# Attention times values for 448 queries in tiles of 128: the last 64 queries of two heads in one stationary operand

## Chip, cores, metric

The kernel runs on one core of a Trainium2 chip. The metric is the device time of a whole execution in microseconds. The kernel before took 406.42 us (median of 4 runs, 406.06 to 406.82). PE is TensorE, PEld its weight loads, DVE VectorE, ACT ScalarE, POOL GpSimd. The kernel places the tiles named `ps_...` and `sc`, which take PE's results here, in PSUM and all other tiles in SBUF.

## The reference

```python
def _attn_ref(q, k, v, tau):                      # 8 x 12 heads, 448 queries, 64 wide
    q_n = q / (norm(q, axis=-1) + 1e-06)
    k_n = k / (norm(k, axis=-1) + 1e-06)
    attn = softmax(q_n @ k_n.T / tau)             # its sum gets + 1e-9
    return attn @ v
# then, on x = (3584 tokens, 768):
    a = x @ w1;  b = x @ w2
    out = ((a * b) @ w3) @ w_out                  # 768 -> 1024 -> 1024 -> 768
```

## The kernel before

Heads are taken in pairs, 48 in all. POOL squares and scales q and k (`sq`, `nrm`), PE transposes them and makes the scores, ACT takes the exponentials, PE multiplies them with the values ("AV"), DVE divides by the row sums, PE transposes back, and the feed-forward part (groups `a`, `b`, `o`) fills PE in between. A planner in the kernel puts all steps in a fixed order per engine, from estimated durations.

AV has the exponentials as the stationary operand, 128 queries at a time, and the values of one head with a column of ones (65 columns) as the moving one. 448 is three and a half times 128, so the fourth tile starts at 320 and computes 64 queries a second time.

```python
QT = (0, 128, 256, S - 128)                       # S = 448, P = 112, NJ = 4, D = 64
...
def scores(pp, half):
    if half == 0:
        exps[pp] = exp_pool.tile([P, NJ, 2, S], BF16, tag="exp", name="expT")
    ...
def exp(pp, c):
    nc.scalar.activation(exps[pp][:, c], scs.pop((pp, c))[:P, :, :S], ACT.Exp,
                         scale=1.0 / float(tau))

def av(pp, hh):
    ...
    ps = psA.tile([128, NJ, D + 1], FP32, tag="av", name="ps_av")
    for m, q0 in enumerate(QT):
        for c in range(NJ):
            nc.tensor.matmul(ps[:, m, :], exps[pp][:, c, hh, q0:q0 + 128],
                             vt[:, 2 * i + hh, c, :], start=(c == 0), stop=(c == NJ - 1))
    ...
def av_norm(pp, hh):
    ps = pav.pop((pp, hh))
    rs = st_pool.tile([128, NJ, 1], FP32, tag="rs", name="rs")
    nc.vector.reciprocal(rs[:, :, 0], ps[:, :, D])
    nc.vector.tensor_mul(osds[pp][:, :, hh, :], ps[:, :, :D],
                         rs.to_broadcast([128, NJ, D]))

def trback(pp):                                   # four transposes into ps_tb
    ...
def tb_copy(pp):
    nc.vector.tensor_copy(xts[b][:, blk, :], pst.pop(("b", pp))[:, 0, :S])
```

Of the kernel before, what the change touches and what calls it, by code (L numbers as in the profile page):

```python
# [8 lines left out]
FP32 = mybir.dt.float32  # L9
BF16 = mybir.dt.bfloat16  # L10
AX = mybir.AxisListType
ALU = mybir.AluOpType
ACT = mybir.ActivationFunctionType
# [6 lines left out]
class Plan:  # L20
# [22 lines left out]
    def add(self, name, on, rank, emit, after=(), takes=(), holds=(), kb=0, later=None,  # L43
            until=None, slack=0.0, port=False):
        self.steps[name] = dict(on=on, rank=rank, emit=emit, after=list(after), later=later,
                                takes=list(takes), kb=kb, until=until, slack=slack, port=port)
        for key in holds:
            self.holders.setdefault(key, []).append(name)
# [79 lines left out]
def kernel(  # L128
# [12 lines left out]
    nc = tc.nc  # L141

    B, H, S, D = q.shape
# [3 lines left out]
    P = 112  # L147
    NJ = S // P
# [5 lines left out]
    KO2 = DF // 128  # L154
    NH = DM // 2
    NP = B * NPAIR
    QT = (0, 128, 256, S - 128)

    ctx.enter_context(tc.manual_schedule())

    const = ctx.enter_context(tc.tile_pool(name="const", bufs=1))
    wpool = ctx.enter_context(tc.tile_pool(name="wpool", bufs=1))
    raw_pool = ctx.enter_context(tc.tile_pool(name="raw", bufs=3))
    sq_pool = ctx.enter_context(tc.tile_pool(name="sq", bufs=3))
    st_pool = ctx.enter_context(tc.tile_pool(name="st", bufs=3))
    nrm_pool = ctx.enter_context(tc.tile_pool(name="nrm", bufs=3))
    head_pool = ctx.enter_context(tc.tile_pool(name="head", bufs=2))
    exp_pool = ctx.enter_context(tc.tile_pool(name="exp", bufs=3))
# [5 lines left out]
    psA = ctx.enter_context(tc.tile_pool(name="psA", bufs=1, space=PSUM))  # L174
# [85 lines left out]
    qks, exps, osds, xts, pst, scs, pav = {}, {}, {}, {}, {}, {}, {}  # L260

    def tr(pp):
        g, i = divmod(pp, GP)
        n = nrms[g]
        ps = psT.tile([128, 2, 512], BF16, tag="tr", name="ps_tr")
        for t in range(2):
            for j in range(NJ):
                nc.tensor.transpose(  # L268
                    ps[:, t, j * P:(j + 1) * P],
                    n[:, i, t, j].rearrange("p h d -> p (h d)"),  # L270
                    ident[:P, :P])
        qks[pp] = head_pool.tile([128, 2, S], BF16, tag="qkT", name="qkT")
        pst[pp] = ps

    def tr_copy(pp):
        nc.vector.tensor_copy(qks[pp], pst.pop(pp)[:, :, :S])  # L276

    def scores(pp, half):
        if half == 0:
            exps[pp] = exp_pool.tile([P, NJ, 2, S], BF16, tag="exp", name="expT")  # L280
        for c in (2 * half, 2 * half + 1):
            sc = psS.tile([128, 2, 512], FP32, tag="sc", name="sc")
            for hh in range(2):
                nc.tensor.matmul(  # L284
                    sc[:P, hh, :S],
                    qks[pp][64 * hh:64 * hh + 64, 1, c * P:(c + 1) * P],
                    qks[pp][64 * hh:64 * hh + 64, 0, :],
                    start=True, stop=True)
            scs[pp, c] = sc

    def exp(pp, c):
        nc.scalar.activation(exps[pp][:, c], scs.pop((pp, c))[:P, :, :S], ACT.Exp,  # L292
                             scale=1.0 / float(tau))

    def av(pp, hh):
        g, i = divmod(pp, GP)
        vt = v_tiles[g % NV]
        ps = psA.tile([128, NJ, D + 1], FP32, tag="av", name="ps_av")
        for m, q0 in enumerate(QT):
            for c in range(NJ):  # L300
                nc.tensor.matmul(  # L301
                    ps[:, m, :],
                    exps[pp][:, c, hh, q0:q0 + 128],
                    vt[:, 2 * i + hh, c, :],
                    start=(c == 0), stop=(c == NJ - 1))
        if hh == 0:
            osds[pp] = head_pool.tile([128, NJ, 2, D], BF16, tag="osd", name="osd")
        pav[pp, hh] = ps

    def av_norm(pp, hh):  # L310
        ps = pav.pop((pp, hh))
        rs = st_pool.tile([128, NJ, 1], FP32, tag="rs", name="rs")
        nc.vector.reciprocal(rs[:, :, 0], ps[:, :, D])  # L313
        nc.vector.tensor_mul(osds[pp][:, :, hh, :], ps[:, :, :D],  # L314
                             rs.to_broadcast([128, NJ, D]))

    def trback(pp):
        b, blk = divmod(pp, NPAIR)
        if blk == 0:
            xts[b] = xpool.tile([128, NPAIR, S], BF16, tag="xT", name="xT")  # L320
        ps = psT.tile([128, 2, 512], BF16, tag="tr", name="ps_tb")
        for m, q0 in enumerate(QT):
            nc.tensor.transpose(  # L323
                ps[:, 0, q0:q0 + 128],
                osds[pp][:, m].rearrange("p h d -> p (h d)"), ident)
        pst["b", pp] = ps

    def tb_copy(pp):
        b, blk = divmod(pp, NPAIR)
        nc.vector.tensor_copy(xts[b][:, blk, :], pst.pop(("b", pp))[:, 0, :S])  # L330

    abts = {}

# [88 lines left out]
    warm_sb = const.tile([128, 512], BF16, name="warm_sb")  # L422
    nc.vector.memset(warm_sb, 0.0)
    ident = const.tile([128, 128], BF16)

    def warm():
        ps = psM.tile([128, 512], FP32, tag="pm", name="ps_warm")
        for _ in range(2):
            nc.tensor.matmul(ps[:, :S], warm_sb[:, :128], warm_sb[:, :S], start=True, stop=True)

    def ones():
        for t in v_tiles:
            nc.gpsimd.memset(t[:, :, :, D:D + 1], 1.0)
# [4 lines left out]
                   exp=3, xT=2, a_sb=KO2, big=1, out_sb=3),  # L438
        begin=dict(PE=1.0, ACT=3.0, DVE=1.2, POOL=1.3))
    add = plan.add  # L440

    add("ident", [("POOL", 0.6)], -90, lambda e: make_identity(nc, ident), later="wo0")
    add("ones", [("POOL", 0.45)], -70, lambda e: ones())
    every = slice(None)
    w3_part = [slice(k, k + 2) for k in range(0, KO2, 2)]
# [10 lines left out]
    for name in loads:  # L456
# [5 lines left out]
        else:  # L462
# [5 lines left out]
            else:  # L468
                i, h0 = "qk".index(what), 2 if g == 0 else 0
# [11 lines left out]
    def chain(what, p, t):  # L481
        return f"{what}{p}.0" if t else f"{what}{p - 1}.1" if p else None
# [8 lines left out]
    for g in range(NG):  # L491
        for i in range(GP):
            p = g * GP + i
            for t in range(2):
# [4 lines left out]
                else:  # L499
# [8 lines left out]
                    holds=[("sq", p, t)], later=chain("sum", p, t),  # L508
# [7 lines left out]
        for i0, i1 in parts:  # L516
            ps = range(g * GP + i0, g * GP + i1)
# [11 lines left out]
    for p in range(NP):  # L529
        g, i = divmod(p, GP)  # L530
        b, blk = divmod(p, NPAIR)
        last = p > 0
        add(f"tr{p}", [("PE", 0.42)], p - 1.2, lambda e, p=p: tr(p),
            [f"scale{p}.0", f"scale{p}.1", "ident"] + ([f"tr{p - 1}"] if last else []),
            [("tr", ("tr", p)), ("qkT", ("qkT", p))], [("nrm", g)],
            slack=0.3 if g > 2 else 0.0)
        add(f"ev{p}", [("DVE", 0.54)], p - 1.1, lambda e, p=p: tr_copy(p), [f"tr{p}"],
            holds=[("tr", p)])
        for h in range(2):
            add(f"sc{p}.{h}", [("PE", 0.6)], p + 0.5 * h - 1, lambda e, p=p, h=h: scores(p, h),  # L540
                [f"ev{p}"] + ([f"sc{p}.0"] if h else [f"sc{p - 1}.1"] if last else []),
                [("sc", ("sc", p, 2 * h)), ("sc", ("sc", p, 2 * h + 1))]
                + ([] if h else [("exp", ("exp", p))]), [("qkT", p)])
            for c in (2 * h, 2 * h + 1):
                add(f"exp{p}.{c}", [("ACT", 0.82)], p + 0.25 * c - 1,
                    lambda e, p=p, c=c: exp(p, c),
                    [f"sc{p}.{h}"] + ([f"exp{p}.{c - 1}"] if c else []), holds=[("sc", p, c)])
        for h in range(2):
            add(f"av{p}.{h}", [("PE", 0.53)], p + 0.5 * h, lambda e, p=p, h=h: av(p, h),
                [f"exp{p}.{c}" for c in range(NJ)] + [f"spread{g}"]  # L550
                + ([f"av{p}.0"] if h else [f"av{p - 1}.1"] if last else []),
                [("av", ("av", p, h))] + ([] if h else [("osd", ("osd", p))]),
                [("exp", p), ("vt", g)])
            add(f"an{p}.{h}", [("DVE", 0.62)], p + 0.5 * h - 0.5,
                lambda e, p=p, h=h: av_norm(p, h), [f"av{p}.{h}"], holds=[("av", p, h)])
        add(f"tb{p}", [("PE", 0.24)], p + 1, lambda e, p=p: trback(p),
            [f"an{p}.0", f"an{p}.1"] + ([f"tb{p - 1}"] if last else []),
            [("tr", ("tb", p))] + ([] if blk else [("xT", ("xT", b))]), [("osd", p)])
        add(f"xt{p}", [("DVE", 0.31)], p - 0.2, lambda e, p=p: tb_copy(p), [f"tb{p}"],
            holds=[("tb", p)])  # L560

    line = []
# [52 lines left out]
    for n in range(60):  # L615
        add(f"warm{n}", [("PE", 0.4)], 10000 + n, lambda e: warm(),
            takes=[("pm", ("warm", n))], later=f"warm{n - 1}" if n else None, until=11.0)
# [39 lines left out]
```

## Time and profile before

| kernel before | |
|---|---|
| time | 406.42 us |
| profiled span, mean granted PE clock | 404.3 us, 0.994 |
| busy PE / DVE / ACT / POOL | 395 / 216 / 248 / 246 us |
| AV matmuls per pair, start to start | 32, 32.5 ns each |
| one exponential (112 x 896) | 916 ns |
| visible PE holes after the first 12 us | 3.4 us in all |

The lines are in the prediction below. How to read them: a group row has the source line, engine, operation, output and inputs, sizes and count, then busy time and the mean of one, then the idle time in front of the group and what ended it. The matmuls of a group overlap in the records (the 16 AV matmuls that start at 209.27 us have a record of 0.68 us, and the next group starts after 0.52), so the cost of a group on PE is the distance from its start to the next start in the timeline. The granted clock is a reading of the profile, as a share of PE's full speed. PE is the bound here (395 of 404.3 us busy), so busy time of another engine matters only where PE waits for it.

### The profile page before, as it was taken

The numbers are of one execution on the slowest core, as the hardware profiler recorded it, in microseconds if no ns is written. First come the engines' busy times: TensorE is split into PE (matmuls) and PEld (weight loads), VectorE is DVE, ScalarE is ACT, GpSimd is POOL, SyncE is SP. The second block draws the span as 40 slices with busy tenths as digits, with TensorE's granted clock in tenths as the row PEclk, the third lists the DMA queues.
The fourth block names the chain that finished last, engine by engine and source line by source line (L and its number), as shares of the span: only waits on it lengthen the run. The fifth ranks groups of instructions, "written<-read, shape, count | busy, mean of one in ns | idle before, by whom it ended". The sixth has DMA issues, their size and how long they took to land.

```text
span 404.3 us, 9387 instructions
## 1 busy us (share of the span) xinstructions
PE 395.0 (98%) x3944; PEld 234.9 (58%) x3944; DVE 216.3 (53%) x484; ACT 247.9 (61%) x399; POOL 245.9 (61%) x258
## 2 busy tenths in 40 slices
PE   8799999999999999999999999999999999999995
PEld 3466665556555666555655566556655566555553
DVE  2785647587576755766655766444344443420310
ACT  3687777766676676757776757566656676323222
POOL 7479899999999999999999999315100000000000
PEclk9899999999999999999999999999999999999999
DMA  8999999256585285753745365000210013103005
GB/s 144 201 206 207 210 199 153 36 70 104 119 102 71 36 153 113 101 68 36 141 82 70 38 106 123 30 2 2 79 39 2 2 41 84 36 0 105 14 5 153
DMA packets 42474, 35.18 MB, mean 87 GB/s; under 512 B 1856, under 2 KB 36416, under 8 KB 42432
## 3 DMA queue, kind: packets, MB, share of 16 engines
q0 software_dynamic: 37312, 23.11, 41.0%
q1 hardware_dynamic: 4752, 11.07, 9.4%
q8 instruction: 31, 0.51, 0.5%
q10 hardware_dynamic: 368, 0.40, 0.3%
q14 instruction: 11, 0.09, 0.1%
HBM read 46.66 MB, written 11.01 MB: 143 GB/s over the span
## 4 chain that ended last, share of the span: by engine, by line
PE 73%; POOL 19%; DMA 3%; issue 2%; DVE 1%; ACT 0%; POOLq 0%; DVEq 0%
PE ps_b L336 15%; PE ps_a L336 14%; PE ps_o L336 14%; PE ps_av L301 10%; PE sc L284 9%; POOL sq L229 8%; POOL nrm L255 7%; PE ps_w L336 5%; PE ps_tr L268 4%; DMA wo_sb<-in_moe_w_out_dram 3%; PE ps_tb L323 2%; POOL raw L198 2%; POOL v_sb L214 2%; PE ps_w L349 1%; POOL w_sb L217 0%
## 5 line engine op out<-in xcount | busy, mean ns | idle before, releaser
L292 ACT ACTIVATE expT<-sc 112x896 bf16<-112x896 f32 x192 | 166.0, 916 | 43.2 <-PE sc L284 42.9
L336 PEld LDWEIGHTS <-w_sb 128*128 128x128 bf16 x768 | 69.6, 98 | 57.2 <-issue 4.1
L255 POOL TENSOR_TENSOR nrm<-raw,rn 112x512 bf16<-112x512 bf16 x90 | 90.8, 1036 | 2.2 <-PE ps_tr L268 2.1
L229 POOL TENSOR_TENSOR sq<-raw 112x512 bf16<-112x512 bf16 x87 | 87.8, 1037 | 0.2
L336 PE MATMUL ps_b<-xT,w_sb 128*128 128x448 bf16 x384 | 83.2, 353 | 0.0
L336 PE MATMUL ps_a<-xT,w_sb 128*128 128x448 bf16 x384 | 83.0, 352 | 0.0
L336 PE MATMUL ps_o<-w_sb,abT 128*128 128x384 bf16 x448 | 80.1, 326 | 0.0
L235 DVE TENSOR_REDUCE ss<-sq 112x8 f32<-112x512 bf16 x96 | 64.0, 679 | 15.2 <-POOL sq L229 14.9
L382 DVE TENSOR_TENSOR abT<-a_sb,ps_b 128x448 bf16<-128x448 bf16 x64 | 39.6, 619 | 57.7 <-PE ps_b L336 54.8
L301 PEld LDWEIGHTS <-expT 112*128 112x128 bf16 x1536 | 59.2, 98 | 19.4 <-issue 8.8
L371 ACT CAST a_sb<-ps_a 128x448 bf16<-128x448 f32 x64 | 34.0, 532 | 52.4 <-PE ps_a L336 51.5
L301 PE MATMUL ps_av<-v_sb,expT 112*128 112x65 bf16 x1536 | 65.2, 194 | 0.0
L284 PE MATMUL sc<-qkT 64*112 64x448 bf16 x384 | 56.9, 374 | 1.4 <-DVE qkT L276 1.3
L336 PEld LDWEIGHTS <-abT 128*128 128x128 bf16 x448 | 41.3, 98 | 26.5 <-issue 2.7
L342 ACT COPY out_sb<-ps_o 128x384 f32<-128x384 f32 x43 | 20.6, 478 | 38.0 <-PE ps_o L336 36.5
L314 DVE TENSOR_TENSOR osd<-ps_av,rs 128x256 bf16<-128x256 f32 x96 | 40.7, 424 | 3.3
L313 DVE RECIPROCAL rs<-ps_av 128x4 f32<-128x4 f32 x96 | 17.1, 178 | 46.2 <-PE ps_av L301 45.9
L214 POOL COPY v_sb<-vraw 112x1536 bf16<-112x1536 bf16 x16 | 23.4, 1460 | 24.4 <-PE ps_av L301 24.0
L276 DVE COPY qkT<-ps_tr 128x896 bf16<-128x896 bf16 x48 | 29.7, 619 | 12.1 <-PE ps_tr L268 12.1
L330 DVE COPY xT<-ps_tb 128x448 bf16<-128x448 bf16 x48 | 18.6, 387 | 20.5 <-PE ps_tb L323 20.2
L284 PEld LDWEIGHTS <-qkT 64*112 64x112 bf16 x384 | 17.3, 125 | 20.7 <-issue 16.4
L268 PEld LDWEIGHTS <-nrm 112*128 112x128 bf16 x384 | 21.9, 99 | 12.1 <-issue 6.6
(37 smaller groups left out, 220.3 us busy)
## 6 DMA issues: line engine op xcount, KB each, us to landing
vraw<-in_v_dram POOLq DMA_DIRECT2D x16, 336.0 KB, 4.8
raw<-in_q_dram POOLq DMA_DIRECT2D x15, 336.0 KB, 5.6
raw<-in_k_dram POOLq DMA_DIRECT2D x15, 336.0 KB, 7.6
w_sb<-in_moe_w_dram POOLq DMA_DIRECT2D x2, 1536.0 KB, 25.4
out_dram<-out_sb SPq DMA_DIRECT2D x7, 336.0 KB, 2.8
out_dram<-out_sb SPq DMA_DIRECT2D x8, 288.0 KB, 3.0
w_sb<-in_moe_w_dram POOLq DMA_DIRECT2D x4, 512.0 KB, 16.2
out_dram<-out_sb SPq DMA_DIRECT2D x8, 240.0 KB, 2.8
```

Source lines behind the costliest of these rows:

```text
L214: nc.gpsimd.tensor_copy(v_tiles[g % NV][:, :, :, :D], vraws.pop(g))
L229: eng.tensor_mul(o, x, x)
L235: nc.vector.reduce_sum(sss[g][:, t, 2 * i:2 * i + 2, :], sqs.pop((g, i, t)), axis=AX.X)
L255: eng.tensor_mul(nrms[g][:, i, t].rearrange("p j h d -> p h j d"), raw_of(g, t, i), rns[g][:, t, 2 * i:2 * i + 2].to_broadcast([P, 2, NJ, D]))
L268: nc.tensor.transpose(ps[:, t, j * P:(j + 1) * P], n[:, i, t, j].rearrange("p h d -> p (h d)"), ident[:P, :P])
L284: nc.tensor.matmul(sc[:P, hh, :S], qks[pp][64 * hh:64 * hh + 64, 1, c * P:(c + 1) * P], qks[pp][64 * hh:64 * hh + 64, 0, :], start=True, s ...
L292: nc.scalar.activation(exps[pp][:, c], scs.pop((pp, c))[:P, :, :S], ACT.Exp, scale=1.0 / float(tau))
L301: nc.tensor.matmul(ps[:, m, :], exps[pp][:, c, hh, q0:q0 + 128], vt[:, 2 * i + hh, c, :], start=(c == 0), stop=(c == NJ - 1))
L314: nc.vector.tensor_mul(osds[pp][:, :, hh, :], ps[:, :, :D], rs.to_broadcast([128, NJ, D]))
L336: nc.tensor.matmul(o, l, r, start=(i == 0), stop=(i == len(pairs) - 1))
L371: nc.scalar.copy(a_sbs[b, fo], pms.pop(("a", b, fo))[:, :S])
L382: nc.vector.tensor_mul(abts[b // 2][:, fo, c0:c0 + S], a_sbs.pop((b, fo)), pms.pop(("b", b, fo))[:, :S])
```

## The change

The intent is to save PE's second computation of 64 queries. Each head keeps three tiles. The last 64 queries of both heads go together, as one stationary operand of 128 columns, against the values of both heads (130 columns). Half of that result is a head's weights on the other head's values and is masked out. To lie side by side for that, the heads are interleaved in the tile of the exponentials; a 0/1 matmul (`fold`) puts the rows back.

```diff
-    QT = (0, 128, 256, S - 128)
+    QT = (0, 128, 256)
+    NM = len(QT)
+    QH = S - 64
...
-            exps[pp] = exp_pool.tile([P, NJ, 2, S], BF16, tag="exp", name="expT")
+            exps[pp] = exp_pool.tile([P, NJ, S, 2], BF16, tag="exp", name="expT")
...
-        nc.scalar.activation(exps[pp][:, c], scs.pop((pp, c))[:P, :, :S], ACT.Exp,
+        nc.scalar.activation(exps[pp][:, c].rearrange("p s h -> p h s"), scs.pop((pp, c))[:P, :, :S], ACT.Exp,
...
-                    exps[pp][:, c, hh, q0:q0 + 128],
+                    exps[pp][:, c, q0:q0 + 128, hh],
...
+        else:
+            for c in range(NJ):
+                nc.tensor.matmul(
+                    ps[:, NM:, :],
+                    exps[pp][:, c, QH:, :].rearrange("p s h -> p (s h)"),
+                    vt[:, 2 * i:2 * i + 2, c, :],
+                    start=(c == 0), stop=(c == NJ - 1))
...
-        nc.vector.reciprocal(rs[:, :, 0], ps[:, :, D])
-        nc.vector.tensor_mul(osds[pp][:, :, hh, :], ps[:, :, :D],
-                             rs.to_broadcast([128, NJ, D]))
+        nc.vector.reciprocal(rs[:, :n, 0], ps[:, :n, D])
+        nc.vector.tensor_mul(osds[pp][:, :NM, hh, :], ps[:, :NM, :D],
+                             rs[:, :NM].to_broadcast([128, NM, D]))
+        if hh:
+            rh = st_pool.tile([128, 2, 1], FP32, tag="rh", name="rh")
+            nc.vector.tensor_mul(rh[:, :, 0], side, rs[:, NM].to_broadcast([128, 2]))
+            nc.vector.tensor_mul(osds[pp][:, NM], ps[:, NM:, :D], rh.to_broadcast([128, 2, D]))
...
+        nc.tensor.matmul(ps[:, 1, :128].bitcast(FP32), osds[pp][:, NM].rearrange("p h d -> p (h d)"),
+                         fold, start=True, stop=True)
...
-        nc.vector.tensor_copy(xts[b][:, blk, :], pst.pop(("b", pp))[:, 0, :S])
+        ps = pst.pop(("b", pp))
+        nc.vector.tensor_copy(xts[b][:, blk, :QH], ps[:, 0, :QH])
+        nc.vector.tensor_copy(xts[b][:, blk, QH:], ps[:, 1, :128].bitcast(FP32))
... (n is NM + hh; osd becomes two fixed tiles, osd_sb; side and fold are made once; the planner's AV, normalisation and copy-back durations change)
```

More of the change, by code (lines that the diff above doesn't have):

```diff
@@ L297, in av @@
         vt = v_tiles[g % NV]
-        ps = psA.tile([128, NJ, D + 1], FP32, tag="av", name="ps_av")
+        ps = psA.tile([128, NM + 2, D + 1], FP32, tag="av", name="ps_av")
         for m, q0 in enumerate(QT):
@@ L306, in av @@
         if hh == 0:
-            osds[pp] = head_pool.tile([128, NJ, 2, D], BF16, tag="osd", name="osd")
+            osds[pp] = osd_tiles[pp % 2]
+        else:
[5 more added lines that the diff above has]
+                    start=(c == 0), stop=(c == NJ - 1))
         pav[pp, hh] = ps
@@ L311, in av_norm @@
         ps = pav.pop((pp, hh))
+        n = NM + hh
         rs = st_pool.tile([128, NJ, 1], FP32, tag="rs", name="rs")
-        nc.vector.reciprocal(rs[:, :, 0], ps[:, :, D])
-        nc.vector.tensor_mul(osds[pp][:, :, hh, :], ps[:, :, :D],
-                             rs.to_broadcast([128, NJ, D]))
+        nc.vector.reciprocal(rs[:, :n, 0], ps[:, :n, D])
[5 more added lines that the diff above has]
+            nc.vector.tensor_mul(osds[pp][:, NM], ps[:, NM:, :D], rh.to_broadcast([128, 2, D]))
     def trback(pp):
@@ L424 @@
     ident = const.tile([128, 128], BF16)
+    fold = const.tile([128, 64], BF16, name="fold")
+    side = const.tile([128, 2], FP32, name="side")
+    osd_tiles = [wpool.tile([128, NM + 1, 2, D], BF16, name=f"osd{i}_sb") for i in range(2)]
     def warm():
@@ L429, in warm, with make_fold @@
             nc.tensor.matmul(ps[:, :S], warm_sb[:, :128], warm_sb[:, :S], start=True, stop=True)
+    def make_fold():
+        sides = ident.rearrange("p (q h) -> p h q", h=2)
+        nc.vector.tensor_add(fold, sides[:, 0], sides[:, 1])
+        nc.vector.reduce_sum(side, sides, axis=AX.X)
     def ones():
@@ L442 @@
     add("ident", [("POOL", 0.6)], -90, lambda e: make_identity(nc, ident), later="wo0")
+    add("fold", [("DVE", 0.35)], -1, lambda e: make_fold(), ["ident"])
     add("ones", [("POOL", 0.45)], -70, lambda e: ones())
@@ L548 @@
         for h in range(2):
-            add(f"av{p}.{h}", [("PE", 0.53)], p + 0.5 * h, lambda e, p=p, h=h: av(p, h),
+            add(f"av{p}.{h}", [("PE", 0.62 if h else 0.4)], p + 0.5 * h, lambda e, p=p, h=h: av(p, h),
                 [f"exp{p}.{c}" for c in range(NJ)] + [f"spread{g}"]
@@ L553 @@
                 [("exp", p), ("vt", g)])
-            add(f"an{p}.{h}", [("DVE", 0.62)], p + 0.5 * h - 0.5,
-                lambda e, p=p, h=h: av_norm(p, h), [f"av{p}.{h}"], holds=[("av", p, h)])
-        add(f"tb{p}", [("PE", 0.24)], p + 1, lambda e, p=p: trback(p),
+            add(f"an{p}.{h}", [("DVE", 0.85 if h else 0.5)], p + 0.5 * h - 0.5,
+                lambda e, p=p, h=h: av_norm(p, h), [f"av{p}.{h}", "fold"], holds=[("av", p, h)])
+        add(f"tb{p}", [("PE", 0.21)], p + 1, lambda e, p=p: trback(p),
             [f"an{p}.0", f"an{p}.1"] + ([f"tb{p - 1}"] if last else []),
             [("tr", ("tb", p))] + ([] if blk else [("xT", ("xT", b))]), [("osd", p)])
-        add(f"xt{p}", [("DVE", 0.31)], p - 0.2, lambda e, p=p: tb_copy(p), [f"tb{p}"],
+        add(f"xt{p}", [("DVE", 0.42)], p - 0.2, lambda e, p=p: tb_copy(p), [f"tb{p}"],
             holds=[("tb", p)])
```

## The prediction

> **What bounds the kernel now.** I read the busy table and the slices of the page first, then the groups by shape, then who waited for whom, then the order of time of TensorE's work. The page begins, and its slices read:
>
> ```profile
> span 404.3 us, 9387 instructions
> PE 395.0 (98%) x3944; PEld 234.9 (58%) x3944; DVE 216.3 (53%) x484; ACT 247.9 (61%) x399; POOL 245.9 (61%) x258
> ...
> PE   8799999999999999999999999999999999999995
> ...
> POOL 7479899999999999999999999315100000000000
> ```
>
> PE has no slice with a hole after the first two; POOL is nearly full from slice 6 to slice 25, then empty. A busy PE is not yet a PE at its pace, because the end of a matmul overlaps the next one. So I took the start-to-start times of its groups from the timeline:
>
> ```profile
> 209.27 0.68 PE L301 MATMUL ps_av<-v_sb,expT 112*128 112x65 bf16 x16
> ...
> 209.79 1.30 PE L336 MATMUL ps_a<-xT,w_sb 128*128 128x448 bf16 x6
> ```
>
> Sixteen AV matmuls take 209.79 - 209.27 = 0.52 us, 32.5 ns each, although the row of the group says 194 ns for one. Over the whole trace an AV group of 16 takes 0.53 us in the median, 0.61 where scores follow it, 53 us for nearly all 96. Four transposes back take 0.23 us (57 ns each), a score group of four 0.52, a transpose group of eight 0.40, a group of six a or b matmuls 1.14, a group of eight out matmuls 1.31. These groups times their counts come to 383 us, and the visible holes after the start are six of 0.2 to 1.3 us. So the span is the sum of TensorE's issue times plus about 20 us of start and end: what the change takes from those issue times it takes from the span, unless it makes PE wait.
>
> The chain of waits passes through POOL (sq 8%, nrm 7% of the span) between 94 and 177 us, where POOL is 96% busy. The table by windows says what that costs there:
>
> ```profile
> 120.00:180.00 60.00, 58.91 (x622) 34.87 (x622) 38.08 (x87) 39.59 (x62) 57.37 (x59) 1.00 0.58 88
> ```
>
> (The columns are the length, then busy PE, PEld, DVE, ACT, POOL.) PE still has 58.9 of 60 us, since the feed-forward groups fill it. The attention follows POOL's pace here, but the order of instructions gives PE other work. DVE has 38.1 of 60: room, but not much.
>
> [...] Nothing in this trace loads weights with a step[...]. [...] 448 and 256 elements of tensor_tensor differ by 619 - 424 = 195 ns, 1.02 ns per element, and bf16 copies of 896 and 448 by 619 - 387 = 232 ns, 0.52 per element.
>
> **The change, part by part.** The rows it touches:
>
> ```profile
> L301 PE MATMUL ps_av<-v_sb,expT 112*128 112x65 bf16 x1536 | 65.2, 194 | 0.0
> ...
> L314 DVE TENSOR_TENSOR osd<-ps_av,rs 128x256 bf16<-128x256 f32 x96 | 40.7, 424 | 3.3
> ...
> L323 PE MATMUL ps_tb<-ident,osd 128*128 128x128 bf16 x192 | 18.8, 220 | 0.8 <-DVE qkT L276 0.7
> L330 DVE COPY xT<-ps_tb 128x448 bf16<-128x448 bf16 x48 | 18.6, 387 | 20.5 <-PE ps_tb L323 20.2
> L313 DVE RECIPROCAL rs<-ps_av 128x4 f32<-128x4 f32 x96 | 17.1, 178 | 46.2 <-PE ps_av L301 45.9
> ```
>
> *AV on PE.* A pair of heads had 32 matmuls of 65 columns: 32 x 32.5 = 1040 ns. It gets 24 of them (780) and four of 130 columns. [...] Sum 1007: only 33 ns saved. Removing a quarter of the matmuls removes little, since the joint ones carry both heads' values and half of their output is thrown away.
> *Back transposes on PE.* Four of 57 ns (228) become three (171)[...]: 200, so 28 ns saved.
> *Sum on PE.* 61 ns per pair, 48 pairs: **2.9 us**, 0.7% of the span.
> *DVE.* Before: 2 x (178 + 424) + 387 = 1591 ns per pair. After: two reciprocals at 178; two products of 192 elements, 424 - 64 x 1.02 = 359 each; one of 128, 294; the tiny side product, some 160 (the fixed part of the tensor_tensor line, 424 - 256 x 1.02 = 163); the copy of 384, 387 - 64 x 0.52 = 354[...]. Sum about 2100, so 0.51 us more per pair, **24 us more DVE work**, from 216 to about 241 us, 60% of the span. This lies beside PE. Where it can reach PE is latency: the second normalisation goes from 0.60 to about 1.0 us, the copy back from 0.39 to 0.57.
> *ACT.* Same 192 exponentials, now written with a step of two elements. I assume 916 ns as now. Even 10% more (17 us over the kernel) would be beside PE.
> *Start.* Two tiny operations build the 0/1 matrices; 0.3 to 0.5 us of DVE early[...].
>
> I compared the orders of TensorE's instructions in both programs and put the measured group times on them. Between the first AV group of a pair and the second lie at least 0.92 us in both (median 1.66 before, 1.31 after), for a normalisation of about 0.57 us. Between the second and the fold the least are 0.52 once and otherwise 1.31 or more, for about 1.0 us. Between the fold and the next user of that PSUM tile at least 0.92, for 0.57. Add 0.2 us for the drain and the signal and most fit; some will not when DVE is busy with a 0.68 us reduction at that moment. The scheduler plans with 0.85 and 0.42 us for the two longer DVE pieces, less than I work out, so its order is a little too tight. I allow 1 us of new PE waits in total: **406.4 - 2.9 + 1.0 = 404.5 us**.
>
> **The rivals.** *1. Stepped weight loads are slower.* All 24 remaining 65-column matmuls of a pair load 128 weights with a step of two elements. [...] Each 10 ns per load is 24 x 48 x 10 ns = 11.5 us. A doubled pace, 65 ns, would cost 37 us and end near 442. A chance of about 22% that it goes over 2% slower this way, and a further tenth for a few ns per load, 406 to 412.
> *2. DVE becomes the wait.* For: 24 us more work in a strict order, 63% busy from 120 to 180 us and about 71% after; PE order too tight; one AV PSUM buffer. Against: the slack above and the same room for two other PSUM tiles. If half of the 48 pairs lost 0.2 us, 5 us: 409.
> *3. The saving is lost to POOL.* From 94 to 177 us the attention follows POOL, so PE gains only if it can fill. Those 83 us hold about 12 pairs, 12 x 61 ns = 0.7 us. This leaves 405.
> *4. The gain is larger than worked out*, if the end of an AV group or the switch to the next weights gets shorter: I see nothing for more than 1 us, 403.5.
>
> **How the range and the chances follow.** About 70% lies around the base case with rivals 2 to 4 mixed in: 402.5 to 408. A tenth lies in the partial loss, to 412; the rest is the slow tail beyond. The range of 8 in 10 is 402.5 to 412. Over 2% faster is below 398.3, which would need three times the PE saving: 1%. Over 2% slower is above 414.5, almost only rival 1: 22%. Within 2%: 77%.
>
> **What would show each step.** A base-case trace has 12 AV matmuls in 0.39 us and the second group in about 0.62 us, a fold group in 0.20 us, DVE near 240 us busy, exponentials at 916 ns and no new PE hole of over 1 us. AV groups of 12 above 0.45 us would show rival 1. PE idle before AV or transposes put down to normalisations or copies back, together over 3 us, would show rival 2. An exponential well over 916 ns would show that the stepped write costs; it would matter only if PE then waited for ACT. What would make the prediction wrong is above all a stepped load at half the pace.

What neither the trace nor a run of this case shows is cut from this text where the marks are: rates of matmuls and weight loads, rules for stepped access, a rate of DVE, and the terms worked out with them. AV came to 1007 ns per pair, of which 780 can be followed (the four joint matmuls are cut); the transposes back to 200, of which 171 can be followed (the fold is cut); DVE to about 2100 (the FP32 copy of 64 is cut). Together they gave the 61 ns per pair, the 2.9 us and the 404.5 us. By my estimate from the same trace, a straight line through its 57 ns for 128 columns and 1.14/6 = 0.190 us for 448 gives 58 ns for a joint matmul of 130 columns and 30 for the fold of 64, and 555 ns less 320 x 1.02 gives 229 for the copy; that leaves 1012 ns, 201 ns and about 2110, so the forecast does not move by more than 0.3 us. For the 0.2 us "for the drain and the signal", the trace has 0.20: the group after the AV group starts at 209.79 us, the reciprocal of its result at 209.99.

## The result, and the profile after

The changed kernel took **431.35 us** (median of 4 runs, 430.1 to 432.78), the kernel before 406.42 beside it. The ratio is 1.0614, 95% interval 1.0579 to 1.065. (Ratios here are the mean time of one kernel's runs over that of the other's of the same rounds, so not quite the ratio of the medians.) Executions over 1.5% slower than the fastest of the same kernel are left out of the means. It is correct, and slower by over 6%; the predicted range ended at 412.

The head of the page and two of its slice rows, changed kernel:

```profile
span 428.0 us, 9167 instructions
PE 401.9 (94%) x3752; PEld 234.0 (55%) x3752; DVE 266.9 (62%) x630; ACT 288.2 (67%) x399; POOL 246.6 (58%) x258
...
PE   8789999999989996979999998999999999999996
...
PEclk9989999999999998998999999999999999999999
```

PE has holes now that it did not have. Its visible holes after the first 12 us are 20.1 us (3.4 before). The mean granted clock is 0.983, not 0.994: besides a stretch near the start and the last microsecond or two, which both kernels have, it was 0.50 for 3.4 us each from 126.6, 164.1 and 191.4 us, just after the three longest holes (1.7, 3.9 and 2.2 us). Three times 3.4 us at half speed are, by my estimate, some 5 us of the span. ACT has 40 us more than before and DVE 51, where 24 had been expected. The window shown in the prediction, 120 to 180 us:

```profile
120.00:180.00 60.00, 53.79 (x517) 30.91 (x514) 46.04 (x97) 40.16 (x56) 48.92 (x50) 0.94 0.50 78
```

PE 53.8 of 60 us and clock 0.94, POOL 48.9 where it had 57.4. The groups by shape tell who has the extra time:

```profile
L294 ACT ACTIVATE expT<-sc 112x896 bf16<-112x896 f32 x192 | 211.4, 1170 | 39.3 <-PE sc L286 38.6
...
L303 PE MATMUL ps_av<-v_sb,expT 112*128 112x65 bf16 x1152 | 54.2, 196 | 2.0 <-ACT expT L294 1.4 <-POOL v_sb L216 0.6
L303 PEld LDWEIGHTS <-expT 112*128 112x128 bf16 x1152 | 48.1, 99 | 20.7 <-issue 8.5 <-ACT expT L294 1.7
L328 DVE TENSOR_TENSOR rh<-side,rs 128x2 f32<-128x2 f32 x48 | 43.9, 915 | 0.0
...
L324 DVE TENSOR_TENSOR osd_sb<-ps_av,rs 128x192 bf16<-128x192 f32 x96 | 34.3, 358 | 3.3
```

The first and third of these rows in the kernel before, from its page:

```profile
L292 ACT ACTIVATE expT<-sc 112x896 bf16<-112x896 f32 x192 | 166.0, 916 | 43.2 <-PE sc L284 42.9
...
L301 PEld LDWEIGHTS <-expT 112*128 112x128 bf16 x1536 | 59.2, 98 | 19.4 <-issue 8.8
```

Two rows are off. The exponential takes 1170 ns, 254 more than before. And the product of two elements takes 915 ns in the mean, more than twice the product of 192 elements under it. The view of the tile `rh` gives the spread (min/median/max in ns):

```profile
L328 DVE TENSOR_TENSOR rh<-side,rs x48: 149/626/5091, 24.1 to 378.7; 128x2 f32<-128x2 f32 x48
```

The longest of them, in the timelines of DVE, POOL and PE:

```profile
158.42 5.09 DVE L328 TENSOR_TENSOR rh<-side,rs 128x2 f32<-128x2 f32 x1
163.54 0.29 DVE L329 TENSOR_TENSOR osd_sb<-ps_av,rh 128x128 bf16<-128x128 f32 x1
...
158.47 5.02 POOL L231 TENSOR_TENSOR sq<-raw 112x512 bf16<-112x512 bf16 x5
...
163.89 0.20 PE L340 MATMUL ps_tb<-fold,osd_sb 128*128 128x64 bf16 x1 [3.91 <-DVE osd_sb L329]
```

The product starts at 158.42, POOL begins five squares at 158.47, and the product ends at 163.51, when POOL ends at 163.49. (Which of the two was really first can't be read: the record of the DVE operation before the product ends only at 158.50.) The normalisation waits behind it, the fold waits for that, and PE stands for 3.91 us. Late in the kernel, where POOL has nothing left:

```profile
358.56 0.15 DVE L328 TENSOR_TENSOR rh<-side,rs 128x2 f32<-128x2 f32 x1
```

I went through all 48. From 323 us on, with POOL quiet, all take 0.15 us. Before that, 32 of 39 take over 0.3 us, and 30 of these end 10 to 27 ns after the end of a POOL product or copy. POOL's own products are not lengthened: the longest is 1061 ns, 1055 in the kernel before. Of what waited for whom, three lines with PE behind DVE; the first and the last wait for the normalisation behind the tiny product:

```profile
PEld L340 <- DVE osd_sb L329: 8.4, 10, 4.1
PE ps_tb L337 <- DVE qkT L278: 7.6, 8, 2.2
...
PE ps_tb L340 <- DVE osd_sb L329: 6.7, 6, 3.9
```

What the prediction feared most, a slow stepped weight load, is not there (timeline of PE, changed kernel):

```profile
208.79 0.55 PE L303 MATMUL ps_av<-v_sb,expT 112*128 112x65 bf16 x12
209.18 0.40 PE L312 MATMUL ps_av<-v_sb,expT 112*128 112x130 bf16 x4
209.50 0.59 PE L286 MATMUL sc<-qkT 64*112 64x448 bf16 x4
```

Twelve matmuls with stepped loads take 209.18 - 208.79 = 0.39 us, 32.5 ns each, as before.

### The profile page after: what moved, and what is told of

Read it like the earlier page. It is cut to its first block, busy times and chain, and to the rows that moved or that the text cites. A ratio compares the mean times of both kernels' runs of the same rounds, so it can differ in the third digit from the quotient of the medians.

```text
span 428.0 us, 9167 instructions
## 1 busy us (share of the span) xinstructions
PE 401.9 (94%) x3752; PEld 234.0 (55%) x3752; DVE 266.9 (62%) x630; ACT 288.2 (67%) x399; POOL 246.6 (58%) x258
## 4 chain that ended last, share of the span: by engine, by line
PE 72%; DVE 17%; ACT 4%; POOL 4%; issue 2%; DVEq 0%; POOLq 0%
PE ps_o L354 16%; PE ps_b L354 14%; PE ps_a L354 14%; PE sc L286 8%; PE ps_av L303 8%; DVE rh L328 7%; PE ps_tr L270 4%; DVE ss L237 3%; ACT expT L294 2%; PE ps_av L312 2%; PE ps_warm L450 2%; PE ps_tb L337 2%; DVE osd_sb L324 2%; PE ps_w L354 2%; DVE abT L400 1%
## 5 line engine op out<-in xcount | busy, mean ns | idle before, releaser
L294 ACT ACTIVATE expT<-sc 112x896 bf16<-112x896 f32 x192 | 211.4, 1170 | 39.3 <-PE sc L286 38.6
L354 PE MATMUL ps_b<-xT,w_sb 128*128 128x448 bf16 x384 | 84.6, 358 | 0.0
L354 PE MATMUL ps_a<-xT,w_sb 128*128 128x448 bf16 x384 | 84.2, 356 | 0.1
L237 DVE TENSOR_REDUCE ss<-sq 112x8 f32<-112x512 bf16 x96 | 62.5, 677 | 1.8 <-POOL sq L231 1.8
L303 PEld LDWEIGHTS <-expT 112*128 112x128 bf16 x1152 | 48.1, 99 | 20.7 <-issue 8.5
L303 PE MATMUL ps_av<-v_sb,expT 112*128 112x65 bf16 x1152 | 54.2, 196 | 2.0 <-ACT expT L294 1.4
L323 DVE RECIPROCAL rs<-ps_av 128x3 f32<-128x3 f32 x96 | 17.2, 180 | 44.5 <-PE ps_av L303 25.4
L328 DVE TENSOR_TENSOR rh<-side,rs 128x2 f32<-128x2 f32 x48 | 43.9, 915 | 0.0
L324 DVE TENSOR_TENSOR osd_sb<-ps_av,rs 128x192 bf16<-128x192 f32 x96 | 34.3, 358 | 3.3
L270 PE MATMUL ps_tr<-ident,nrm 112*128 112x112 bf16 x384 | 27.7, 217 | 1.5 <-DVE xT L348 1.5
```

The costliest lines, as they stand in the source:

```text
L237: nc.vector.reduce_sum(sss[g][:, t, 2 * i:2 * i + 2, :], sqs.pop((g, i, t)), axis=AX.X)
L270: nc.tensor.transpose(ps[:, t, j * P:(j + 1) * P], n[:, i, t, j].rearrange("p h d -> p (h d)"), ident[:P, :P])
L294: nc.scalar.activation(exps[pp][:, c].rearrange("p s h -> p h s"), scs.pop((pp, c))[:P, :, :S], ACT.Exp, scale=1.0 / float(tau))
L303: nc.tensor.matmul(ps[:, m, :], exps[pp][:, c, q0:q0 + 128, hh], vt[:, 2 * i + hh, c, :], start=(c == 0), stop=(c == NJ - 1))
L324: nc.vector.tensor_mul(osds[pp][:, :NM, hh, :], ps[:, :NM, :D], rs[:, :NM].to_broadcast([128, NM, D]))
L328: nc.vector.tensor_mul(rh[:, :, 0], side, rs[:, NM].to_broadcast([128, 2]))
```

## The experiments

Theory R: DVE's tiny product, with two operands in SBUF, is held up by POOL, and PE waits behind it. Theory E: the longer exponentials hold up what else needs ACT, and PE waits for that. Kernels are compared only within the same rounds.

| run | change | ratio to before (95%) |
|---|---|---|
| e1_rh_fused | changed kernel, tiny product folded away | 1.0028 (0.9967 to 1.0089) |
| e2_exp_flat | changed kernel, exponentials unstepped, result wrong | 1.1066 (1.1024 to 1.1107) |
| e3_before_step | kernel before, stepped exponentials and loads | 1.0070 (1.0025 to 1.0114) |
| e4_before_rh | kernel before, tiny product added | 1.0873 (1.0823 to 1.0923) |
| e6_rh_psum | changed kernel, one operand in PSUM | 0.9984 (0.9951 to 1.0016) |
| e11_before_psum | kernel before, tiny product, one operand in PSUM | 1.0015 (0.9982 to 1.0048) |
| e8_fused_flat | e1, unstepped, wrong | 0.9981 (0.9962 to 0.9999) |
| e1b_fused | e1 again | 0.9985 (0.9954 to 1.0016) |
| e5_replan | e1, planned on measured durations | 1.0279 (1.0238 to 1.0321) |
| e9_plan_dve | e1, only DVE's durations | 0.9977 (0.9953 to 1.0000) |
| e10_plan_exp | e1, only the exponential's | 1.0267 (1.0248 to 1.0285) |
| e9b_plan_dve | e9 again, 5 rounds | 1.0014 (0.9978 to 1.0050) |

**e1_rh_fused.** The mask becomes the second operand of the large product:

```diff
-            nc.vector.tensor_mul(rh[:, :, 0], side, rs[:, NM].to_broadcast([128, 2]))
-            nc.vector.tensor_mul(osds[pp][:, NM], ps[:, NM:, :D], rh.to_broadcast([128, 2, D]))
+            nc.vector.scalar_tensor_tensor(osds[pp][:, NM], ps[:, NM:, :D], rs[:, NM],
+                side.rearrange("p (h o) -> p h o", o=1).to_broadcast([128, 2, D]),
+                op0=ALU.mult, op1=ALU.mult)
```

> The changed kernel with the tiny side product (2 elements, both operands in SBUF, 915 ns mean, up to 5.09 us while POOL runs) folded into the product after it (one operand in PSUM, one in SBUF); all else as in the changed kernel. Theory R (the tiny product is held up by POOL, and DVE, then PE, wait behind it): no DVE operation beyond 0.7 us any more, DVE busy falls by about 40 us to 225, the PE holes of over 0.6 us go, time 405 to 411. Theory E (the exponentials, now 1170 ns because they write with a step, hold the roots, POOL and the scores up): stays at 425 or more. If both carry it: 412 to 422.

Measured: 408.74 us, the kernel before 409.0 beside it. Group row of the new operation, and the page's busy line:

```profile
PE 394.0 (97%) x3752; PEld 232.1 (57%) x3752; DVE 225.9 (56%) x579; ACT 287.7 (71%) x402; POOL 246.0 (61%) x258
...
L327 DVE SCALAR_TENSOR_TENSOR osd_sb<-ps_av,rs,side 128x128 bf16<-128x128 f32 x48 | 16.4, 341 | 0.0
```

The exponentials are as long as in the changed kernel (ACT 287.7 us), yet the whole loss is gone. DVE has 41 us less. This is theory R's number, and theory E cannot give it.

Two things of the expectation did not come. The new product has two inputs from SBUF, not one: `side`, and `rs` as one value per partition. It took 341 ns in the mean of 48 here, and 340 to 343 ns in e1b, the same kernel (tile view), so `rs` in this form did not bring the hold-up back. And one DVE operation still went beyond 0.7 us: six products `nrm`, which both kernels run on DVE near the start, have both operands in SBUF. In the kernel before all six took 679 to 693 ns; here one took 1.85 us, beside a copy on POOL (timelines of DVE and POOL, e1):

```profile
19.03 1.85 DVE L257 TENSOR_TENSOR nrm<-raw,rn 112x512 bf16<-112x512 bf16 x1
...
18.84 1.48 POOL L216 COPY v_sb<-vraw 112x1536 bf16<-112x1536 bf16 x1
```

**e2_exp_flat.**

```diff
-        nc.scalar.activation(exps[pp][:, c].rearrange("p s h -> p h s"), ...
+        nc.scalar.activation(exps[pp][:, c].rearrange("p s h -> p (s h)").rearrange("p (h s) -> p h s", h=2), ...
```

> The changed kernel with the exponentials written without a step into the same tile (the two heads one after the other, so the AV reads mix heads: the result is wrong on purpose, every instruction and size otherwise the same). Both theories: the exponential back to about 916 ns. Theory R: the tiny product still takes several us at times, time 424 to 431. Theory E: time 405 to 412. If both carry it: 414 to 422.

Measured: 450.71 us, slower than the changed kernel, which no theory expected. Its rows of the exponential and of the tiny product:

```profile
L294 ACT ACTIVATE expT<-sc 112x896 bf16<-112x896 f32 x192 | 165.7, 915 | 56.4 <-PE sc L286 56.3
...
L328 DVE TENSOR_TENSOR rh<-side,rs 128x2 f32<-128x2 f32 x48 | 59.3, 1235 | 0.0
```

With the exponentials back at 915 ns the hold-ups became longer: 1235 ns in the mean, against 915. Theory E is out as the main cause. That shorter exponentials shift POOL's rows against the tiny products, and so lengthen the hold-ups, is my reading of it; no run isolates that.

**e3_before_step.**

```diff
-            exps[pp] = exp_pool.tile([P, NJ, 2, S], ...        +  [P, NJ, S, 2]
-        nc.scalar.activation(exps[pp][:, c], ...               +  exps[pp][:, c].rearrange("p s h -> p h s")
-                    exps[pp][:, c, hh, q0:q0 + 128],           +  exps[pp][:, c, q0:q0 + 128, hh]
```

> The kernel before with the two heads interleaved in the exponential's tile and nothing else: exponentials write with a step of two elements, all 32 AV weight loads of a pair read with a step of two. Weight loads: no change, 0.52 us per AV group of 16. Exponential about 1170 ns, ACT busy about 297 us. Theory R: the longer exponentials are beside PE, time 406 to 410. Theory E: 418 to 430.

Measured: 411.05 us against 409.0, 0.7% more.

```profile
L292 ACT ACTIVATE expT<-sc 112x896 bf16<-112x896 f32 x192 | 211.6, 1172 | 29.3 <-PE sc L284 28.6
...
L301 PEld LDWEIGHTS <-expT 112*128 112x128 bf16 x1536 | 59.8, 98 | 21.5 <-issue 8.1 <-ACT expT L292 2.0 <-DVE osd L314 1.7
```

The step alone makes the exponential 1172 ns and leaves the loads at 98 ns and an AV group of 16 at 0.52 us. Forty-six us more of ACT cost about 3 us of time here: nearly all of it lies beside PE.

**e4_before_rh.**

```diff
         nc.vector.reciprocal(rs[:, :, 0], ps[:, :, D])
+        if hh:
+            r2 = st_pool.tile([128, NJ, 1], FP32, tag="rh", name="rh")
+            nc.vector.tensor_mul(r2[:, :, 0], rs[:, :, 0], one4)      # one4: ones, in SBUF
+            rs = r2
```

> The kernel before with one tiny product of 4 elements, both operands in SBUF (reciprocals by one), put between the reciprocal and the product of the second head, once per pair, and nothing else. Theory R: the tiny product takes 0.15 us with POOL quiet and up to several us beside POOL's products, PE gets holes before the transposes, time 416 to 432. Theory E: 406 to 409.

Measured: 443.83 and 444.83 us in its two fast runs, against 409.0 (the other two of its four runs were slow, 452.55 and 457.9). Forty-eight products of four elements, which change no number, cost 8.7%, some 36 us. The profile that was taken fell in a slow run, 452.55 us; its row and its tile view have the same shape as in the changed kernel:

```profile
L316 DVE TENSOR_TENSOR rh<-rs,one 128x4 f32<-128x4 f32 x48 | 57.2, 1191 | 1.7
...
L316 DVE TENSOR_TENSOR rh<-rs,one x48: 161/322/7443, 25.4 to 397.3; 128x4 f32<-128x4 f32 x48
```

The cost is larger than I expected for theory R (416 to 432), but the direction and the mechanism are its own.

**e6_rh_psum and e11_before_psum** ask whether it is the two operands in SBUF, or one more short step as such. The reciprocal is written a second time, in place into PSUM, and read from there, so each has even one DVE operation per pair more than its partner. The edit of e6 (e11 does the same in the kernel before, on four elements):

```diff
-            nc.vector.tensor_mul(rh[:, :, 0], side, rs[:, NM].to_broadcast([128, 2]))
+            nc.vector.reciprocal(ps[:, NM:, D], ps[:, NM:, D])
+            nc.vector.tensor_mul(rh[:, :, 0], side, ps[:, NM:, D])
```

> The changed kernel with one operand of the tiny product moved to PSUM: a second tiny reciprocal is written in place into the PSUM accumulator and the side product reads it there, so there is one more DVE operation per pair, but none with both operands in SBUF. If it is the two SBUF operands that let POOL hold it up: the tiny product takes 0.15 to 0.25 us always, PE holes of over 0.7 us go, time 406 to 412 like the fused form. If it is the extra short operation as such, or its place in DVE's order: 425 to 435.

> The control to the kernel before with the tiny product: the same tiny product of 4 elements at the same place, but with one operand in PSUM (a second tiny reciprocal is written there first, so there are two more DVE operations per pair, not one). If only two SBUF operands are held up by POOL: the tiny product takes 0.15 to 0.2 us always, time within 1% of the kernel before. If any extra step between reciprocal and product does the harm: 1.05 or more, as the run with both operands in SBUF (1.087).

Measured: 408.45 us and 409.33 us, both the same as the kernel before. Tile views of e6 and of e11:

```profile
L329 DVE TENSOR_TENSOR rh<-side,ps_av x48: 156/156/158, 25.7 to 347.9; 128x2 f32<-128x2 f32 x48
```

```profile
L317 DVE TENSOR_TENSOR rh<-one,ps_av x48: 157/159/159, 28.5 to 351.3; 128x4 f32<-128x4 f32 x48
```

Moving one operand to PSUM takes the spread from 149 to 5091 ns down to 156 to 158, with POOL just as busy. This settles the cause for these short products: not the step, not its place, but two tensor inputs from SBUF beside POOL (1.0614 and 1.0873 of the kernel before with both in SBUF, 0.9984 and 1.0015 with one in PSUM). All of POOL's products and copies here read SBUF; no run tries one that only writes.

**e8_fused_flat and e1b_fused**: the base case of the prediction, without hold-up and without step (wrong result; the edit is e2's on top of e1's), and its yardstick.

> The fused form (no tiny product) with the exponentials written without a step: wrong result on purpose, all instructions and sizes otherwise the same. This is the base case of the prediction, with neither hold-up nor step. If the rest of the working was right, it is 0.5 to 1% below the kernel before and about 2 us below the fused form: ratio 0.990 to 0.996. If something else takes the PE saving: ratio 1.0.

> The fused form again, the same kernel as in the first job, beside the other three on one chip: about 1.003 of the kernel before, exponentials 1170 ns. It is the yardstick for the two runs before it.

Measured: 408.19 and 408.15 us, against 408.83. So in the fused form the step costs nothing that these runs can show (e3 has 0.7% for it in the kernel before), and the base case is not 0.5 to 1% faster either: 0.2%. The saving on PE had to be looked for. From the starts in the traces, all AV groups together took 53.9 us before and 53.8 in e9b (the same instructions as e1), the transposes back with the fold 11.2 and 9.8. So 1.5 us are saved of the 2.9 worked out, and AV saves next to nothing: per pair 0.39 + 0.395 + 0.237 us without the switch to scores, against 2 x 0.52, which is 18 ns and not 33. Against that stand longer visible holes after the first 12 us, 5.8 to 6.0 us in e1, e1b and e9b against 3.4 (7.0 in e8), most of them before 70 us; in e9b they are mostly behind DVE's copies and normalisations. So 1.5 us saved and some 2.5 us of new holes come out even within the noise.

**e5_replan, e9_plan_dve, e10_plan_exp, e9b_plan_dve** try to get those holes back by planning with measured durations.

```diff
-            on exp: [("ACT", 0.82)]                    +  1.1              (e5, e10)
-            on an:  [("DVE", 0.85 if h else 0.5)]      +  0.97 / 0.57      (e5, e9)
-            on xt:  [("DVE", 0.42)]                    +  0.57             (e5, e9)
```

> The fused form with the order planned on the measured durations (exponential 1.10 us from start to start, normalisations 0.57 and 0.97, copy back 0.57) and not on the planner's old ones: right result, same instructions, another order. If part of the fused form's loss to the base case is an order that is too tight: 1 to 3 us faster than the fused form, ratio to before 0.992 to 1.0. If not: as the fused form, within 0.5%.

> The fused form with only the planner's VectorE durations corrected (normalisations 0.57 and 0.97, copy back 0.57). The run with all durations corrected came out 2.8% over the kernel before, against the expectation. If the VectorE numbers did that: 1.02 to 1.03 of before. If the exponential's number did: 0.995 to 1.003, as the fused form.

> The fused form with only the planner's exponential corrected (1.10 us in place of 0.82). If this number made the replanned order slow (the attention is planned later, POOL gets its buffers later, 'POOL waits for AV' grows from 22 us to over 40): 1.02 to 1.03 of before. If the VectorE numbers did: 0.995 to 1.003.

> The fused form with the planner's VectorE durations corrected, again, with more rounds: the best right version so far (0.9977, interval 0.9953 to 1.0). If its small gain is real: 0.995 to 0.999 of the kernel before. If it was noise: an interval around 1.0.

Measured: e5 420.61 us, a miss: 2.8% slower. e9 and e10 divide it: the exponential's truer duration alone does it (420.07 us), DVE's do no harm. Windows of e10, 20 to 60 and 60 to 120 us, and one of its waits:

```profile
20.00:60.00 40.00, 37.98 (x380) 24.18 (x380) 25.69 (x60) 27.88 (x43) 34.26 (x36) 0.91 1.27 205
60.00:120.00 60.00, 55.52 (x544) 33.21 (x545) 39.79 (x101) 43.49 (x59) 55.97 (x58) 0.91 0.63 92
```

```profile
POOL v_sb L216 <- PE ps_av L312: 48.2, 6, 13.5
```

The clock is 0.91 in both windows (e9b: 0.96 and 1.00), PE has more holes (11.8 us after the first 12), and POOL waits 48 us for AV to release a buffer where e1b waits 22. Why a truer number gives an order this much worse stays open. e9 (407.9 us) looked 0.2% better than the kernel before; e9b (408.5 us), with five rounds, has 1.0014 and an interval around 1. No version here beats the kernel before by more than the noise.

## Why the prediction was wrong

- **The bound** was right: PE's issue times and holes make the span. The 23.7 us between the two spans are 16.7 us of visible holes and, by the estimate from the clocks above, 5 us at a granted clock of 0.50; the rest is not assigned.
- **The step that failed** is the term "the tiny side product, some 160" in the sum for DVE, with the sentence after it, "This lies beside PE". With POOL quiet the product takes 149 ns, so the size was right for an idle neighbour. With POOL's work beside it, it took 915 ns in the mean of all 48 and up to 5.09 us, 43.9 us in all where the term gives 7.7. The rest of that sum held: the other DVE rows of the change add up to 92.9 us, worked out 93. I took the 160 ns from a row whose product has one operand in PSUM and did not ask where this one's operands lie. e1, e4, e6 and e11 show it from four sides.
- **Rival 2** named the right engine, but as a question of total work and a tight order, with 5 us for it. It was hold-up: e1 has 226 us of DVE and no loss, the changed kernel 267. The sign that the prediction gave for rival 2 (over 3 us of PE idle behind normalisations or copies back) did come, with 6.7 us before the fold alone, but it cannot tell the two causes apart; e6, with one DVE operation more and no loss, does.
- **Rival 1**, which held nearly all of the chance for "slower", did not happen at all: 0.39 us for twelve stepped loads' matmuls, as the base case said. So "over 2% slower" came, but not for the reason that its 22% stood on.
- **The exponential** was assumed at 916 ns and took 1170, 28% or 0.28 ns per element more, where I had allowed for 10%. That it lies beside PE held: 0.7% in e3, nothing visible between e8 and e1b.
- **The PE saving** of 2.9 us was mis-sized: about 1.5, the transposes' part right (1.4), AV's near nothing. The four joint matmuls took 59 ns each, where the line through the trace before gives 58. The allowance of 1 us for new waits was about 2.5. By the ratios of the fused form (e1b 0.9985, e1 1.0028) the change without the hold-up would lie at 405.8 to 407.6 beside the 406.42, inside the predicted range but not at 404.5.

## What to carry to other kernels

Before adding a DVE operation beside a busy POOL, look at where its inputs lie: a product of two elements with both inputs in SBUF cost some 25 us in the changed kernel, one of four elements 36 in e4, and the same two with an input from PSUM cost nothing that the runs show (0.9984 and 1.0015 of the kernel before). In the profile the sign was an operation whose maximum was 34 times its minimum at one shape (5091 and 149 ns; 46 times in e4); look then at what the other engine starts and ends with it. Before removing redundant matmuls, compare the columns that the replacement streams: four of 130 columns took 0.237 us, the time of about seven of 65 at 32.5 ns, so four of them in place of eight of 65 saved almost nothing (18 ns per pair).
